# Three small moves in the front of a fused attention and mixer kernel: one weight tile's loads a step sooner, one batch's correction written ahead of two copies, and one product placed in another PSUM bank

## The chip, the cores and the metric

The kernel runs on one core of one Trainium2 chip. The metric is device time in microseconds (us) of one execution, and the median of three runs is used. One further execution was recorded by the hardware profiler; every row of the profile comes from that one, and its own time differs a little from the median (table below).

The core has engines that run independently and meet at semaphores: TensorE (PE, with its weight loads shown as PEld), VectorE (DVE), ScalarE (ACT), GpSimd (POOL) and SyncE (SP, which here only issues DMAs; ScalarE issues a few as well). Each engine takes its instructions in the order in which they were written, so an instruction that waits holds all that stand behind it on its engine.

## The reference, cut to what matters

```python
for b in range(nb):                       # lightning attention, heads of 64
    intra = einsum('bhic,bhjc->bhij', qb, kb) * Dmask
    intra = einsum('bhij,bhjd->bhid', intra, vb)
    inter = einsum('bhid,bhde->bhie', qb * lam_pow, kv_state)
    out[:, :, sl] = intra + inter
    kv_state = lam_block * kv_state + einsum('bhsd,bhse->bhde', kb * rev_pow, vb)
x = out as (B, S, H*D)                    # 4 x 768 x 512
h = (x.T @ U @ V).T                       # U: 768 x 32, V: 32 x 768, fp64 inputs
u = x + h
return u + relu(u @ w_ch1) @ w_ch2        # w_ch1: 512 x 2048, w_ch2: 2048 x 512
```

There are four batches, eight heads of 64 and 768 positions. The weights of the mixer come as 64-bit floats; the kernel turns their words into 32-bit floats with integer and float instructions of VectorE and ScalarE, and splits each into a high part, a low part and a difference, so that three products in the matmul's faster format stand for one exact one.

## The kernel before, in words

**Steps.** The attention goes by steps `s` = 0 to 23: batch `b` = s // 6 and chunk `c` = s % 6 of 128 positions. Every step is a list of pieces (`step`, L656 to L681), and this list is the order of the work: it is written out by hand, and each piece puts its instructions on the queues of several engines. For a step in the middle the pieces are, in order:

- `mix` and `turn` of an earlier batch's chunk (its correction h, and its transposition for the mixer), and `split` (the parts of the transposed chunk);
- `prep(s+1)`: PE transposes the next chunk's q and k into the PSUM tile `pqk` (L361), ScalarE copies them out as `qt` and `kt` (L367), and SP loads a further q;
- `scale(s+1)`: GpSimd multiplies q by powers of lam (L392) and the next k by others (`ks`, L381);
- `mixed` (VectorE adds h to x, L574) and `late` (ScalarE's share of the weight work);
- `intra(s)` (PE, masked scores by v into `px`, L455), `state(s)` (PE, `ks` by v into `pkv`, L427, and VectorE's new state `kv`, at a first chunk a plain copy, L433), a load of v on ScalarE's queue, and `inter(s)` (PE adds q by the state to `px`, L466; ScalarE copies `px` out as `x_nat`, L472). At c = 0 there is no state yet, so `inter` is the copy alone;
- `scores(s+1)` (PE, L408) and `masked(s+1)` (VectorE, L417), with the step's share of weight work, `aside(s)`, between them;
- `store` of a finished chunk and the load of a further k, both on SP.

**PSUM.** The front uses tiles of two banks of 512 floats per partition each: tags `pqk`, `px`, `pss` and `pm`, one buffer each. `px` holds 256 columns of 512 in each of its two banks. The product `pkv` borrows a tile (L423): `pm` up to s = 6, later `pss` at chunks 2 to 4, and `pqk` at chunks 0 and 1. In `pqk` it has to wait for ScalarE's copies of q and k.

**The correction h.** After a batch's last chunk PE computes x by U for the batch (`low`, L482) and ScalarE copies the sum out as `p_f` (L491). `next_of_low` is then called twice in the next batch's first step. The first call (`own`, L525) rounds four strips of `p_f` into `vp` on ScalarE (L528) and takes the rest on GpSimd (L529); in the list it stands behind `prep`, so behind the copies of q and k on ScalarE. The second call (`other`) sends four small DMAs from `vp` to `vp` on SP (L539). `mix` (L562) multiplies V by `vp`; the first `mix` of a batch is due in the next step, at c = 1, behind `inter`. For the last batch there is another path after the attention.

**Weight work.** `side` (L738 to L747) lists at which step each instruction group of the first weight tiles is written: U, V, and the first two of 16 tiles of w_ch1. A tile of w_ch1 has twelve groups: four fetches of 128 KB each on SP (L146), `one` (exponents, L166, with two ScalarE instructions), `mantissa` (L155), `two` (L184), `three` (L192), `four` (L197) and three for the split. The groups of one step go into `aside(s)`, after `scores(s+1)` and ahead of `masked(s+1)`, so what VectorE has there stands ahead of the mask. The first tile has its fetches at steps 8 to 11 and `one` at 12. The second has

```python
(w1_steps(1, True, True), (15, 16, 17, 18, 18, 22, 23, NS, NS, NS, NS, NS)),
```

that is fetches at 15, 16, 17 and 18, and `one` at 18 too. The buffer of the words alternates between two pools, so the second tile's fetches don't wait for the first tile's groups.

**After the attention** come the products with w_ch1 (`hidden`, L833 and L844) for the rest of the weight tiles, with results parked in DRAM, and then the products with w_ch2 (L965 to L969). They take the time from about 120 us to the end, with PE busy throughout.

Of the kernel before, what the change touches and what calls it, by code (L numbers as in the profile page):

```python
# [18 lines left out]
def kernel(  # L19
# [30 lines left out]
    B, H, S, D = q.shape  # L50
    HP = H // 2
    NT = S // P
# [7 lines left out]
    NS = B * NT  # L60
# [142 lines left out]
    def split_steps(tile_of, src, in_parts=False, scale=None, apart=False):  # L203

        st = {}

        def dst():
            if "w" not in st:
                st["w"] = wconv.tile([P, C], FP32, tag="wf", name="wf")
            return st["w"]  # L210

        def five():
            st["o"] = o = tile_of()
            st["t"] = o[:, 0, :].bitcast(FP32)
            on_scalar(lambda: nc.scalar.mul(o[:, 0, :], st["w"], NEAR))  # L215

        def six():
            w, low = st["w"], st["o"][:, 1, :]
            st["low"] = low.bitcast(FP32) if scale is None else w
            nc.vector.tensor_tensor(  # L220
                out=low if scale is None else w, in0=w, in1=st["t"], op=ALU.subtract
            )
            if scale is not None:
                on_scalar(lambda: nc.scalar.mul(low, w, scale))

        def seven():
            nc.vector.scalar_tensor_tensor(
                st["o"][:, 2, :], st["t"], -E, st["low"], ALU.mult, ALU.add
            )

        return weight_steps(dst, src, C, in_parts=in_parts, apart=apart) + [five, six, seven]
# [3 lines left out]
    def w1_steps(ft, in_parts=False, apart=False):  # L235
        def tile_of():
            w1v[ft] = w1_pool.tile([P, 3, C], F32R, tag="w1", name="w1")
            return w1v[ft]

        cols = moe_w_ch1[:, ft * P : (ft + 1) * P].rearrange("(c p) f -> p c f", p=P)  # L240
        return split_steps(tile_of, cols, in_parts, apart=apart)
# [13 lines left out]
    def two_banks(name, tag):  # L255
        return psf.tile([P, 2, N], FP32, tag=tag, name=name)
# [81 lines left out]
    st = {}  # L338
# [80 lines left out]
    def state(s):  # L419
        c = s % NT  # L420
        if c < NT - 1:
            ks, vr = st[s]["ks"], raw[s, "v"]
            pkv = two_banks("pkv", "pm" if s <= NT else "pss" if c > 1 else "pqk")[:, 0, 0 : HP * D]  # L423
            pkv = pkv.rearrange("p (a e) -> p a e", a=HP)
            for a in range(HP):
                for x in range(2):
                    nc.tensor.matmul(  # L427
                        out=pkv[half[x], a, :], lhsT=ks[:, a, x, :], rhs=vr[:, 2 * a + x, :],
                        start=True, stop=True,
                    )  # L430
            kv[s + 1] = att.tile([P, HP, D], FP32, tag="kv", bufs=2, name="kv")
            if c == 0:
                nc.vector.tensor_copy(out=kv[s + 1], in_=pkv)  # L433
            elif c > 1:
                nc.vector.tensor_tensor(out=kv[s + 1], in0=pkv, in1=st[s]["faded"], op=ALU.add)
            else:
                for a in range(HP):
                    nc.vector.scalar_tensor_tensor(
                        kv[s + 1][:, a, :], kv[s][:, a, :], lamc[:, a, :], pkv[:, a, :],
                        ALU.mult, ALU.add,  # L440
                    )
# [207 lines left out]
    for s in range(NS):  # L649
        b, c = divmod(s, NT)  # L650
        done = s - NT - 1
        more = s + 1 < NS
        turns = done > 0 and (done - 1) // TG < FG
        mixes = 0 <= done < NS - NT - 1
        rows = c == 0 and b > 0
        step = [("fade", s)] * (c > 0)  # L656
        step += [("mix", done)] * (mixes and c != 1) + [("turn", done - 1)] * turns
        step += [("split", done - 1)] * turns
        step += [("prep", s + 1)] * more
        step += [("mix", done + 1)] * (not more)  # L660
        step += [("next_of_low", b - 1)] * rows
        step += [("scale", s + 1)] * more
        step += [("mixed", done)] * (mixes and c != 1)
        step += [("late", s - 1)] * (1 < s < NT - 1 or s > NT)
        step += [("turned", done - 2)] * (done > 1 and c == 1)
        step += [("mixed", done + 1)] * (not more)
        both = [("intra", s), ("state", s)]
        step += (both if s > NT else both[::-1]) + [("next_v", s), ("inter", s)]
        step += [("next_of_low", b - 1)] * rows
        step += [("late", s)] * (s < 2 or s in (NT - 1, NT))  # L670
        step += [("turned", done - 1)] * (done > 0 and c > 0)
        step += [("mix", done), ("mixed", done)] * (mixes and c == 1)
        step += [("scores", s + 1)] * more
        step += [("low", b)] * (more and c == NT - 1)
        step += [("aside", s)] * (0 < s < NT - 2 or s > NT)
        step += [("masked", s + 1)] * more
        step += [("low_rows", b)] * (more and c == NT - 1)
        step += [("aside", s)] * (s in (0, NT - 2, NT - 1, NT))
        step += [("store", done)] * (done >= 0 and done // TG < FG)
        step += [("next_k", s)] * (s > 0)  # L680
        pieces += step  # L681
    waiting = {name: list(range(NS)) for name in "qkv"}

    def load_next(name, engine=nc.sync):
# [4 lines left out]
    run = {  # L689
        "prep": prep, "fade": fade, "scores": scores, "masked": masked, "inter": inter,  # L690
        "intra": intra, "state": state,
        "low": low, "low_rows": low_rows, "next_of_low": next_of_low, "mix": mix, "turn": turn,
        "mixed": mixed, "store": store, "next_v": next_v, "split": lambda s: splits.pop(s)(),
# [3 lines left out]
    def v_steps():  # L697

        st = {}

        def dst():
            if "v" not in st:
                st["v"] = wconv.tile([P, C], FP32, tag="wf", name="vf")[0 : 2 * R, 0:SH]
            return st["v"]

        def parts(gs):
            for half in range(2):
                rows, cols = slice(half * R, (half + 1) * R), slice(half * SH, (half + 1) * SH)
                for g in gs:
                    yield v_hl[g * R : (g + 1) * R, cols], rows  # L710

        def five():
            st["t"] = t = wconv.tile([P, C], FP32, tag="wt", name="vt")[0 : 2 * R, 0:SH]
            nc.vector.tensor_scalar(
                t.bitcast(U32), st["v"].bitcast(U32), HI, None, ALU.bitwise_and
            )
            on_scalar(high)

        def high():
            for out, rows in parts((0, 2)):  # L720
                nc.scalar.copy(out, st["t"][rows])

        def low(g, engine):
            for out, rows in parts((g,)):
                engine.tensor_tensor(
                    out=out, in0=st["v"][rows], in1=st["t"][rows], op=ALU.subtract
                )

        halves = [moe_V[:, half * SH : (half + 1) * SH] for half in range(2)]
        return weight_steps(dst, halves, SH, 2 * R, in_parts=True) + [  # L730
            five, lambda: low(1, nc.vector), lambda: low(3, nc.gpsimd),
        ]
# [6 lines left out]
    for steps, at in (  # L739
        (u_side, (-1, 1, 1, 2, 2)),  # L740
        (v_steps(), (0, 0, 3, 3, 4, 4, 4, 5, 5)),
        (w1_steps(0, True, True), (8, 9, 10, 11, 12, 14, 15, 16, 17, 17, 20, 21)),
        (w1_steps(1, True, True), (15, 16, 17, 18, 18, 22, 23, NS, NS, NS, NS, NS)),
    ):
        assert len(steps) == len(at)
        for step, n in zip(steps, at):
            side.setdefault(n, []).append(step)  # L747
# [140 lines left out]
    c0, b = NS - NT, B - 1  # L888
# [180 lines left out]
```

## Time and profile before

| | us |
|---|---|
| median of 3 runs | 659.63 |
| lowest and highest run | 659.31, 661.56 |
| the profiled execution's own time | 657.43 |
| its span, first to last instruction | 655.6 |
| PE busy | 640.6 (98%) |
| VectorE busy | 435.8 (66%) |
| ScalarE busy | 268.6 (41%) |
| GpSimd busy | 116.4 (18%) |

A row of the timeline reads: start in us, length in us, engine, line, operation, output <- inputs, shape, count, and in brackets how long the engine had been idle before it and what ended that. "SPq" and "ACTq" are instructions that issue DMAs. A row of waits reads: engine, line, what it waited for, us in total, times, and the longest. In a table of stretches PEclk is the mean share of full speed that PE's clock had in the records.

### The profile page before, as it was taken

What the parts mean: (1) busy time and instruction counts of PE and PEld (TensorE: products, weight loads), DVE (VectorE), ACT (ScalarE), POOL (GpSimd) and SP (SyncE); (2) the same over time, 40 slices, a digit from 0 to 9 for tenths busy, and PEclk for the clock granted to TensorE, in tenths of its full rate; (3) what the DMA queues carried; (4) which work ended last, traced back from release to release, by engine and by line L of the source; (5) the groups of instructions that cost most, each with busy time, mean ns of one, the idle gap of its engine ahead of it and who ended that gap; (6) DMA issues with size and microseconds to landing.
All of it is one profiled execution on the core that took longest, in us unless ns stands there. A gap on an engine that the chain in (4) does not pass through costs nothing.

```text
span 655.6 us, 13402 instructions
## 1 busy us (share of the span) xinstructions
PE 640.6 (98%) x5242; PEld 539.5 (82%) x5242; DVE 435.8 (66%) x713; ACT 268.6 (41%) x497; POOL 116.4 (18%) x104
## 2 busy tenths in 40 slices
PE   8999979999999999999999999999999999999997
PEld 7889968778888888888888888888888888888886
DVE  6766857676997777777798244585575665855854
ACT  4666756434664444444455131332232322322320
POOL 4475966331000000000000000030030210300300
PEclk9999998999999999999999999999999999999999
DMA  9989995155787556555576999865363363453521
GB/s 227 241 197 259 236 239 130 50 201 170 262 287 253 211 210 211 209 212 210 211 253 255 332 323 379 292 216 173 98 215 108 116 211 97 147 176 94 180 81 64
DMA packets 132737, 131.69 MB, mean 201 GB/s; under 512 B 81538, under 2 KB 90754, under 8 KB 132674
## 3 DMA queue, kind: packets, MB, share of 16 engines
q1 hardware_dynamic: 107552, 124.41, 58.4%
q10 hardware_dynamic: 25122, 6.42, 4.4%
q8 instruction: 41, 0.67, 0.4%
q14 instruction: 22, 0.18, 0.1%
HBM read 80.09 MB, written 50.33 MB: 199 GB/s over the span
## 4 chain that ended last, share of the span: by engine, by line
PE 93%; DVE 2%; DMA 1%; ACT 1%; issue 1%; POOL 0%; SPq 0%; ACTq 0%; DVEq 0%
PE pz L833 26%; PE pz L965 13%; PE pz L967 13%; PE pd L969 13%; PE pd L844 13%; PE px L455 3%; PE pss L408 3%; PE px L466 2%; PE pqk L361 1%; PE pkv L427 1%; PE pm L562 1%; DMA qraw<-in_q_dram 1%; PE pp L482 1%; PE pm L625 1%; DMA vp<-vp 0%
## 5 line engine op out<-in xcount | busy, mean ns | idle before, releaser
L833 PE MATMUL pz<-u_hl,w 128*128 128x512 f32 x768 | 184.5, 390 | 0.0
L833 PEld LDWEIGHTS pz<-u_hl,w 128*128 128x128 f32 x768 | 143.7, 188 | 30.0 <-ACT r L840 0.3
L967 PE MATMUL pz<-w_hl,m 128*128 128x512 f32 x384 | 148.6, 389 | 0.0
L965 PE MATMUL pz<-w_hl,m 128*128 128x512 f32 x384 | 148.2, 389 | 0.0
L969 PE MATMUL pd<-w_d,m 128*128 128x512 f32 x384 | 147.4, 389 | 0.0
L948 ACT ACTIVATE m<-rm 128x512 fp32r<-128x512 f32 x96 | 60.6, 632 | 183.1 <-PE pd L969 122.9
L949 DVE SCALAR_TENSOR_TENSOR m<-rm,m 128x512 fp32r<-128x512 f32 x96 | 71.5, 747 | 96.0 <-ACT m L948 96.0
L994 POOL TENSOR_TENSOR o<-o,u 128x512 f32<-128x512 f32 x20 | 29.7, 1521 | 433.3 <-DVE o L990 433.3
L849 DVE SCALAR_TENSOR_TENSOR r<-pd,r 128x512 f32<-128x512 f32 x96 | 61.7, 685 | 60.4 <-ACT r L840 48.2
L844 PE MATMUL pd<-u_d,w 128*128 128x512 f32 x384 | 95.9, 390 | 0.0
L969 PEld LDWEIGHTS pd<-w_d,m 128*128 128x128 f32 x384 | 72.1, 188 | 15.4 <-DVE m L950 0.3
L967 PEld LDWEIGHTS pz<-w_hl,m 128*128 128x128 f32 x384 | 72.1, 188 | 15.1
L965 PEld LDWEIGHTS pz<-w_hl,m 128*128 128x128 f32 x384 | 72.1, 188 | 14.7
L844 PEld LDWEIGHTS pd<-u_d,w 128*128 128x128 f32 x384 | 71.9, 188 | 14.8
L840 ACT ACTIVATE r<-pz 128x512 f32<-128x512 f32 x96 | 51.7, 590 | 64.4 <-PE pz L833 64.4
L950 DVE SCALAR_TENSOR_TENSOR m<-m 128x512 fp32r<-128x512 f32 x96 | 74.7, 780 | 3.0
L417 DVE TENSOR_TENSOR sm<-pss,mask 128x512 f32<-128x512 f32 x48 | 30.9, 684 | 16.7 <-PE pss L408 16.7
L215 ACT ACTIVATE w<-wf 128x512 fp32r<-128x512 f32 x32 | 20.3, 634 | 38.6 <-DVE wf L197 30.7
L455 PE MATMUL px<-vraw,sm 128*64 128x64 f32 x768 | 28.7, 229 | 5.6 <-issue 5.5
L455 PEld LDWEIGHTS px<-vraw,sm 128*64 128x64 f32 x768 | 25.8, 141 | 7.3 <-issue 5.8
L173 ACT ACTIVATE sc<-sc,ends 128x512 f32<-128x512 uint32 x30 | 21.6, 720 | 22.8 <-DVE sc L166 22.8
L408 PE MATMUL pss<-qt,kt 64*128 64x128 f32 x384 | 28.8, 289 | 0.0
(89 smaller groups left out, 608.5 us busy)
## 6 DMA issues: line engine op xcount, KB each, us to landing
r_d<-r SPq DMA_DIRECT2D x96, 256.0 KB, 2.4
rm<-r_d SPq DMA_DIRECT2D x96, 256.0 KB, 2.7
words<-in_moe_w_ch_dram SPq DMA_DIRECT2D x30, 512.0 KB, 4.3
w_d<-w SPq DMA_DIRECT2D x16, 768.0 KB, 3.4
w_hl<-w_d SPq DMA_DIRECT2D x16, 512.0 KB, 5.8
u_d<-x_nat SPq DMA_DIRECT2D x24, 256.0 KB, 4.0
u<-u_d SPq DMA_DIRECT2D x24, 256.0 KB, 4.3
qraw<-in_q_dram SPq DMA_DIRECT2D x23, 256.0 KB, 4.8
```

The lines of the kernel that those rows point to most:

```text
L408: nc.tensor.matmul(out=pss[:, x, a, :], lhsT=kt[half[x], a, :], rhs=qt[half[x], a, :], start=True, stop=True,)
L455: nc.tensor.matmul(out=px[half[t], x, a, :], lhsT=sm[:, x, a, half[t]], rhs=vr[:, 2 * a + x, :], start=(a == 0), stop=(alone and a == HP - 1),
L833: nc.tensor.matmul(out=like(acc[g][0], g), lhsT=w[:, n, ct, :], rhs=columns(uhl[g][:, n], g, ct), start=(ct == 0 and n == 0), stop=(ct == ...
L840: nc.scalar.mul(rs[g], acc[g][0], 4096.0 + 1.0)
L844: nc.tensor.matmul(out=like(acc[g][1], g), lhsT=w[:, 2, ct, :], rhs=columns(ud[g], g, ct), start=(ct == 0), stop=(ct == CT - 1),)
L849: nc.vector.scalar_tensor_tensor(rs[g], acc[g][1], 4096.0, rs[g], ALU.mult, ALU.add)
L948: nc.scalar.activation(out=m[:, 0], in_=r, func=AF.Relu, scale=NEAR)
L949: nc.vector.scalar_tensor_tensor(m[:, 1], r, 0.0, hi, ALU.max, ALU.subtract)
L950: nc.vector.scalar_tensor_tensor(m[:, 2], hi, E, low, ALU.mult, ALU.subtract)
L965: nc.tensor.matmul(out=pz, lhsT=m[:, 0, cols], rhs=hl[:, 0], start=first, stop=False)
L967: nc.tensor.matmul(out=pz, lhsT=m[:, 1, cols], rhs=hl[:, 1], start=False, stop=end)
L969: nc.tensor.matmul(out=pd, lhsT=m[:, 2, cols], rhs=dd, start=first, stop=end)
```

## The change

Three edits. (A) At the first chunk of the third and fourth batch (s = 12 and 18) `pkv` is written to the unused columns 256 to 511 of the first bank of `px`, in place of a tile with the tag `pqk`. (B) At s = 6 the first call of `next_of_low` is written ahead of `prep(7)` rather than behind it; at s = 12 and 18 it stays where it was. (C) The second tile's four fetches are written at steps 14, 15, 16 and 17 rather than 15 to 18; `one` stays at 18.

```diff
         if c < NT - 1:
             ks, vr = st[s]["ks"], raw[s, "v"]
-            pkv = two_banks("pkv", "pm" if s <= NT else "pss" if c > 1 else "pqk")[:, 0, 0 : HP * D]
+            if c == 0 and s > NT:
+                pkv = st[s]["px"][:, 0, HP * D : 2 * HP * D]
+            else:
+                tag = "pm" if s <= NT else "pss" if c > 1 else "pqk"
+                pkv = two_banks("pkv", tag)[:, 0, 0 : HP * D]
             pkv = pkv.rearrange("p (a e) -> p a e", a=HP)
...
         step += [("split", done - 1)] * turns
+        step += [("next_of_low", b - 1)] * (s == NT)
         step += [("prep", s + 1)] * more
         step += [("mix", done + 1)] * (not more)
-        step += [("next_of_low", b - 1)] * rows
+        step += [("next_of_low", b - 1)] * (rows and s > NT)
         step += [("scale", s + 1)] * more
...
-        (w1_steps(1, True, True), (15, 16, 17, 18, 18, 22, 23, NS, NS, NS, NS, NS)),
+        (w1_steps(1, True, True), (14, 15, 16, 17, 18, 22, 23, NS, NS, NS, NS, NS)),
```

## The prediction

> **What bounds the kernel now.** I read the busy times first, then the waits of PE in the front (20 to 120 us), then the timeline around each of these waits.
>
> ```profile
> PE 640.6 (98%) x5242; PEld 539.5 (82%) x5242; DVE 435.8 (66%) x713; ACT 268.6 (41%) x497; POOL 116.4 (18%) x104
> ...
> PE px L455 <- issue: 5.5, 3, 4.8
> PE pm L562 <- DMA vp<-vp: 1.2, 1, 1.2
> PE pkv L427 <- issue: 0.3, 2, 0.2
> ```
>
> PE is busy for 640.6 us of the 655.6 us span, so nearly only PE's idle time, or time in which it runs slowly, is there to be won. The three wait rows come from the answer on PE's waits between 20 and 120 us, and they are in effect the three edits: up to 4.8 us ahead of one `intra` (edit C), 1.2 us in the first `mix` (edit B), two stalls of about 0.2 us ahead of `pkv` (edit A). Behind the front PE hardly waits, so I take it that what the front gains arrives at the end undiminished: the products that follow hang on PE and on engines that move with it, not on a fixed hour.
>
> **Edit A, `pkv` into `px`'s bank at s = 12 and 18.** No instruction is added or taken away; the eight matmuls no longer wait for the copy `kt`.
>
> ```profile
> 63.83 0.59 ACT L367 COPY kt<-pqk 128x512 f32<-128x512 f32 x1
> ...
> 64.52 0.69 PE L427 MATMUL pkv<-vraw,ks 128*64 128x64 f32 x16 [0.19 <-issue]
> ...
> 65.25 0.42 DVE L433 COPY kv<-pkv 128x256 f32<-128x256 f32 x1 [0.53 <-PE pkv L427]
> ...
> 65.66 0.59 ACT L472 COPY x_nat<-px 128x512 f32<-128x512 f32 x1
> ...
> 67.14 1.24 PE L455 MATMUL px<-vraw,sm 128*64 128x64 f32 x32
> ...
> 69.50 0.78 PE L562 MATMUL pm<-vp 64*128 64x256 f32 x4
> ...
> L539 SPq DMA_DIRECT2D vp<-vp x1: 585/585/585, 67.8 to 67.8; - x1
> ...
> DMA to landing us min/median/max: 1.8/1.8/1.8
> ...
> 91.94 0.69 PE L427 MATMUL pkv<-vraw,ks 128*64 128x64 f32 x16 [0.16 <-issue]
> ```
>
> At s = 12 `kt` ends at 63.83 + 0.59 = 64.42 and `pkv` starts at 64.52 after 0.19 us of idling; at s = 18 it idled 0.16 us. If everything behind moved along, A would bring 0.35 us. But what is late next stands in the same rows: `mix` at 69.50 needs four strips of `vp`. The last strip's DMA (the answer on the tile `vp`) starts at 67.8 and lands 1.8 us later, at 69.6, so `mix` begins with the strip not quite there and takes 0.78 us. The strips hang on ScalarE behind `kt`, which A does not move. I take 0 for A. Ends: a gain of 0.35 and a loss of 0.1, the latter since the changed `pkv` shares `px`'s bank, so ScalarE's `x_nat` (65.66) now also waits for VectorE's copy `kv`, which ends at 65.25 + 0.42 = 65.67. Behind it on ScalarE stand the next split and the next copies of q and k; the next writer of `px` comes only at 67.14, 0.9 us after `x_nat` ends at 66.25.
>
> [...]
>
> **Edit B, ScalarE's four casts ahead of `qt` and `kt` at s = 6.** The four casts move past two copies on ScalarE; GpSimd's four subtractions and SP's four DMAs keep their places in their queues but are released sooner.
>
> ```profile
> 34.39 0.27 ACT L491 COPY p_f<-pp 128x128 f32<-128x128 f32 x1
> ...
> 35.03 0.58 ACT L367 COPY qt<-pqk 128x512 f32<-128x512 f32 x1 [0.37 <-PE pqk L361]
> ...
> 35.51 0.59 ACT L367 COPY kt<-pqk 128x512 f32<-128x512 f32 x1
> ...
> 36.12 0.62 ACT L528 CAST vp<-p_f 32x128 fp32r<-32x128 f32 x2
> ...
> 36.41 1.16 PE L408 MATMUL pss<-qt,kt 64*128 64x128 f32 x16
> 36.50 2.02 POOL L529 TENSOR_TENSOR vp<-p_f,vp 32x128 fp32r<-32x128 f32 x4 [2.03 <-ACT vp L528]
> ...
> 36.97 2.79 SPq L539 DMA_DIRECT2D vp<-vp  x4
> ...
> 39.17 3.01 DMA vp<-vp
> ...
> 40.05 0.69 PE L466 MATMUL px<-kv,qs 64*64 64x64 f32 x32
> ...
> 42.23 0.50 PE L562 MATMUL pm<-vp 64*128 64x256 f32 x3 [1.17 <-DMA vp<-vp]
> ```
>
> (The row without an engine is from the chain of work that ended last.) `p_f` ends at 34.66. Today the casts follow `kt` and start at 36.12; then they start at about 34.68. Two take 0.62 us, so the first is done at 34.99 and the four at 35.93. GpSimd's chain starts at 35.05 rather than 36.50, 1.45 us sooner, and with it SP's DMAs: the last strip, which today is on its way from 39.17 to 42.18, would land at about 40.73.
>
> The price: `qt` starts at 35.95 rather than 35.03, `kt` follows 0.48 us later as it does today (35.03 to 35.51) and ends at 35.95 + 0.48 + 0.59 = 37.02. `scores(7)`, which PE began at 36.41, now waits for `kt` until about 37.05: 0.64 us lost, and everything of the step behind it moves by that. `inter(7)`, today 40.05 to 40.74, then ends at 41.38. By then the strips are there, so `mix` runs through; four of its matmuls need about 0.4 us (today's last three took 0.50 with their loads) and it ends at 41.78 rather than at 42.73. Gain: 42.73 - 41.78 = 0.95 us; I take 0.9. Ends: 1.58 us if `scores(7)` is not held (0.95 + 0.64), and a loss of 0.64 us if the strips land later by as much as PE comes later, which could only come from SP's queue, where the load of q that `prep(7)` issues stands ahead of them. GpSimd's next product, q by powers, is queued behind the subtractions: they end at 35.05 + 2.02 = 37.07 and `qt` at 36.53, both ahead of today's 38.52.
>
> **Edit C, the second tile's fetches one step sooner.** One DMA of 128 KB leaves step 18 and one joins step 14; nothing else moves. At s = 18 `one` stands on VectorE directly behind the last fetch's own step, and ahead of `masked(19)`.
>
> ```profile
> 92.66 0.42 DVE L433 COPY kv<-pkv 128x256 f32<-128x256 f32 x1 [0.53 <-PE pkv L427]
> ...
> 94.04 0.42 PE L361 MATMUL pqk<-ident,kraw 64*128 64x64 f32 x8
> ...
> 95.64 0.58 SPq L146 DMA_DIRECT2D words<-in_moe_w_ch_dram  x1
> ...
> 98.10 0.43 DVE L166 TENSOR_SCALAR sc<-words 128x512 uint32<-128x512 uint32 x1 [5.01 <-DMA words<-in_moe_w_ch_dram]
> 98.44 1.28 DVE L417 TENSOR_TENSOR sm<-pss,mask 128x512 f32<-128x512 f32 x2
> ...
> 99.23 1.98 PE L455 MATMUL px<-vraw,sm 128*64 128x64 f32 x32 [4.76 <-issue]
> ...
> 94.50:99.20 4.70, 0.00 (x0) 0.00 (x1) 1.10 (x3) 1.72 (x4) 3.20 (x3) 0.74 0.63 173
> 99.20:103.60 4.40, 4.37 (x84) 4.17 (x86) 1.98 (x6) 1.22 (x3) 1.46 (x2) 0.51 0.43 97
> ...
> 70.03 1.14 PE L408 MATMUL pss<-qt,kt 64*128 64x128 f32 x16
> ...
> 103.61 1.06 PE L408 MATMUL pss<-qt,kt 64*128 64x128 f32 x16
> ...
> L146 SPq DMA_DIRECT2D words<-in_moe_w_ch_dram x1: 2170/2170/2170, 86.0 to 86.0; - x1
> ...
> DMA to landing us min/median/max: 6.1/6.1/6.1
> ```
>
> VectorE is done with `kv` at 93.08. Its next instruction, L166, needs words whose fetch SP issues only at 95.64, behind the four strips; they land at 98.10. The mask (98.44) is queued behind L166, and `intra(19)` behind the mask, so PE, which finished its transposes at 94.46, starts at 99.23. The stretch from 94.50 to 99.20 has no PE work at all (the columns are length, busy time of PE, PEld, DVE, ACT and POOL, then PEclk, DMA share and GB/s). It has a second cost: in the next 4.4 us PEclk is 0.51, and `intra` takes 1.98 us where the same 32 matmuls took 1.24 us at s = 13.
>
> With C the last fetch is the one written at step 17. The fetch there today starts at 86.0 and lands 6.1 us later, at 92.1 (the last two rows of the fence), ahead of 93.08, so L166 does not wait. VectorE then does L166 until 93.5, and the mask can start when `scores(19)` ends.
>
> For the size I lay step 18 beside step 12, which has the same pieces and `one` of the first tile at the same place, with its words already landed. From `pkv` to the `scores` two steps on: 64.52 to 70.03 is 5.51 us at s = 12, and 91.94 to 103.61 is 11.67 us at s = 18. The difference, 6.16 us, is idle time (99.23 - 94.46 = 4.77) and half clock (the rest, 1.39). What is late next is again `mix`: the last strip of `vp`, whose row shows
>
> ```profile
> L539 SPq DMA_DIRECT2D vp<-vp x2: 585/585/585, 94.3 to 95.0; - x2
> ...
> DMA to landing us min/median/max: 1.9/2.0/2.1
> ```
>
> starts at 95.0 and lands by 97.1. At s = 12 `mix` came 69.50 - 64.52 = 4.98 us behind `pkv`, which gives 96.92 here; a wait of up to 0.2 us. I take 6.1 us. Ends: 4.77 us if the half clock came anyway, 6.3 us with A's share on top. On SP the store and the loads behind the fetch in step 18 go out sooner; in step 14 a store and a load of k go out later by its issue, 2.2 us where the row shows one (2170 ns). The loads are two steps and more ahead of their use, which hides it as in steps 15 to 17; without that cover it is the last rival below.
>
> **The sum.** 0 + 0.9 + 6.1 = 7.0 us. The profiled execution would take 657.43 - 7.0 = 650.4 us. It is 2.2 us below the median of the runs; against the median the forecast is 659.63 - 7.0 = 652.6 us. The ends add up to 4.77 - 0.64 - 0.1 = 4.0 us (655.6) and 6.3 + 1.58 = 7.9 us (651.7; A's gain is in the 6.3 for one of its two places and doubtful at the other).
>
> **The rivals.**
>
> *B brings nothing.* If `scores(7)` loses its 0.64 us and the strips come no sooner than 42.18, `mix` ends where it ended, and 6.1 us remain: 653.5. For it: ScalarE's queue is the only thing I moved, and SP's DMAs take 2.79 us for four. Against it: GpSimd's chain had waited for the casts alone.
>
> *The half clock stays out of the sum.* The clock's halving may not have been in the runs of the median: then C is worth 4.77 and the sum is 5.7, 654.0. Against it: the profiled execution, which has the half clock, is faster than the median. [...] The trace agrees that a pause of 4.77 us is followed by 0.51; no run here shows one that is not.
>
> *The pause moves.* If the mask comes early but `vp`'s strips, now with PE right behind them, or the loads of q and k land some 3 us later than read, C is worth about 3 us: 655.7.
>
> *The edits do nothing.* If L166 waits as long for another of the four fetches, only B is left: 658.7. The rows speak against it: the third fetch lands at 92.1.
>
> *Slower: the DMA engines become the bound in steps 14 to 17.*
>
> ```profile
> 72.30:76.60 4.30, 4.30 (x128) 4.06 (x126) 3.98 (x7) 3.16 (x9) 4.30 (x5) 1.00 1.13 269
> ...
> qraw<-in_q_dram SPq DMA_DIRECT2D x23, 256.0 KB, 4.8
> ...
> words<-in_moe_w_ch_dram SPq DMA_DIRECT2D x8, 128.0 KB, 5.1
> ```
>
> In the stretch of step 14 the DMA share is 1.13 at 269 GB/s. Each step has three loads and a store of the size in the q row, 256 KB, about 1.05 MB in 4.3 us. With 128 KB more (the last row), a step of 1.18 MB takes 4.4 us at that rate, 0.1 us more, and the loads run ahead by two steps or more, so nothing shows. To end 0.5% slower than before, these four steps would have to lose 7.0 + 3.3 = 10.3 us, 2.6 us each: 1.18 MB in 6.9 us, 171 GB/s. From that rate down it decides, and the time is 663 or more. [...]
>
> **How the numbers follow.** Forecast 0.70 (its own range 650.8 to 654.4, from the ends of B and A and the spread of the runs); B nothing 0.13; half clock out 0.05; pause moved 0.06; nothing 0.03; slower 0.03. About 0.5% (3.3 us) is what a measurement of this kernel can tell from no change. Faster by more, below 656.3: the first four, 0.94, from which I keep back 0.02 for their ends; same 0.05; slower 0.03. The range goes from 650.2, the upper sum of 7.9 with the 1.5 us that the median may come nearer to the profiled execution's time, to 655.8, which takes in the third rival.
>
> **What would show it.** After: no idle of PE above 0.5 us between 90 and 105; L166 of the second tile without a wait; PEclk near 1.00 there; `scores(7)` about 0.6 us later, `mix` of s = 7 without the 1.2 us; at s = 12 and 18 no idle before L431 but a `mix` that waits for `vp`. I would be wrong if VectorE's L166 still waits, if PE's wait for `vp` at s = 7 stays, or if waits for loads of q, k or v appear in steps 14 to 20.

## The result, and the profile after

| us | before | after |
|---|---|---|
| median of 4 runs each | 660.60 | 650.76 |
| lowest and highest run | 659.31, 662.20 | 649.45, 651.64 |
| the profiled execution's own time | 657.43 | 651.64 |
| its span | 655.6 | 649.8 |

The changed kernel takes 0.9848 of the time before, with a 95% interval of 0.9817 to 0.9879. The forecast was 652.6 us, a ratio of 0.9893 to its median of 659.63. The two profiled executions lie closer together than the medians, 5.8 us apart; what is in these 5.8 us stands in the section on why the prediction was right. The median of 650.76 us lies at the lower end of the forecast: just below its own range of 650.8 to 654.4, and above the lower end of the whole range, 650.2.

The page of the profile after has these lines of busy time and of PE's clock (40 slices of the span, nine tenths and more in every one), and PE's waits between 20 and 120 us (columns: engine, line, what it waited for, us in total, times, the longest):

```profile
PE 639.3 (98%) x5242; PEld 538.5 (83%) x5242; DVE 435.9 (67%) x713; ACT 268.1 (41%) x497; POOL 116.6 (18%) x104
...
PEclk9999999999999999999999999999999999999999
...
PE px L470 <- issue: 1.5, 2, 0.8
PE px L459 <- issue: 0.7, 2, 0.4
PE pkv L431 <- issue: 0.6, 2, 0.3
PE pss L408 <- ACT kt L367: 0.4, 1, 0.4
```

Gone are the two large waits of before, 4.8 us ahead of an `intra` and 1.2 us for `vp`. What is left are pieces of 0.8 us and less. The largest, in `inter` (L470), is new.

**Step s = 6 and 7 (edit B).** The timeline after:

```profile
34.27 1.26 ACT L532 CAST vp<-p_f 32x128 fp32r<-32x128 f32 x4
...
34.65 2.15 POOL L533 TENSOR_TENSOR vp<-p_f,vp 32x128 fp32r<-32x128 f32 x4 [0.97 <-ACT vp L532]
...
35.16 1.10 PE L459 MATMUL px<-vraw,sm 128*64 128x64 f32 x32
35.24 3.02 SPq L543 DMA_DIRECT2D vp<-vp  x4
...
36.04 0.59 ACT L367 COPY kt<-pqk 128x512 f32<-128x512 f32 x1
...
36.68 1.16 PE L408 MATMUL pss<-qt,kt 64*128 64x128 f32 x16 [0.42 <-ACT kt L367]
...
40.94 0.50 PE L566 MATMUL pm<-vp 64*128 64x256 f32 x4
...
41.28 1.05 PE L408 MATMUL pss<-qt,kt 64*128 64x128 f32 x16
```

And two rows of before that weren't shown, the `intra` of s = 6 and the `scores` of s = 8:

```profile
35.38 1.10 PE L455 MATMUL px<-vraw,sm 128*64 128x64 f32 x32
...
42.46 1.16 PE L408 MATMUL pss<-qt,kt 64*128 64x128 f32 x16
```

The four casts now run in one go from 34.27, ahead of `kt`, which ends at 36.63; `scores(7)` waits 0.42 us for it. In return `mix` (40.94) has all its strips and runs through, four matmuls in 0.50 us, and `scores(8)` starts at 41.28 rather than at 42.46.

**Steps s = 12 and 18 (edits A and C).** The timeline after:

```profile
63.44 0.63 PE L431 MATMUL px<-vraw,ks 128*64 128x64 f32 x15
...
68.36 0.61 PE L566 MATMUL pm<-vp 64*128 64x256 f32 x4
...
68.72 1.13 PE L408 MATMUL pss<-qt,kt 64*128 64x128 f32 x16
...
91.31 1.15 PE L459 MATMUL px<-vraw,sm 128*64 128x64 f32 x32
...
92.29 0.64 PE L431 MATMUL px<-vraw,ks 128*64 128x64 f32 x16
...
93.32 0.42 DVE L166 TENSOR_SCALAR sc<-words 128x512 uint32<-128x512 uint32 x1
...
94.07 1.29 DVE L417 TENSOR_TENSOR sm<-pss,mask 128x512 f32<-128x512 f32 x2 [0.33 <-PE pss L408]
...
94.25 0.57 ACT L476 COPY x_nat<-px 128x512 f32<-128x512 f32 x1
...
94.87 1.09 PEld L459 LDWEIGHTS px<-vraw,sm 128*64 128x64 f32 x32 [0.24 <-ACT x_nat L476]
...
96.37 0.69 PE L431 MATMUL pkv<-vraw,ks 128*64 128x64 f32 x16 [0.28 <-issue]
...
97.61 0.51 PE L566 MATMUL pm<-vp 64*128 64x256 f32 x4
...
97.96 1.05 PE L408 MATMUL pss<-qt,kt 64*128 64x128 f32 x16
```

Both `pkv` (63.44 and 92.29) start without idle time. L166, `one` of the second tile, no longer waits for its words, and the mask follows at 94.07. Two small waits are new: `intra(19)` at 94.87 for `x_nat`, 0.24 us, and the next `pkv` at 96.37, 0.28 us. Four stretches of the profile after follow; the last two are the ones that the prediction shows of before (length, busy time of PE, PEld, DVE, ACT, POOL, then PEclk, DMA share, GB/s):

```profile
80.00:84.00 4.00, 3.25 (x93) 2.97 (x90) 2.33 (x4) 1.50 (x3) 3.49 (x3) 1.00 1.01 265
84.00:88.00 4.00, 3.27 (x98) 2.93 (x96) 3.78 (x5) 1.91 (x4) 2.80 (x3) 1.00 1.15 295
94.50:99.20 4.70, 4.32 (x114) 3.85 (x111) 3.21 (x9) 4.57 (x11) 4.55 (x6) 1.00 0.72 173
99.20:103.60 4.40, 4.40 (x131) 4.16 (x130) 3.53 (x7) 2.93 (x8) 4.40 (x4) 1.00 1.10 274
```

Where PE stood idle for 4.70 us from 94.50 on and then ran at 0.51 of its clock, it is busy for 4.32 of 4.70 us, at full clock. In the first two stretches, steps 16 and 17, PE lacks 0.7 us each. These are the pauses of `inter`:

```profile
82.20 0.68 PE L470 MATMUL px<-kv,qs 64*64 64x64 f32 x26 [0.76 <-issue]
...
87.32 0.34 PE L470 MATMUL px<-kv,qs 64*64 64x64 f32 x7 [0.73 <-issue]
```

They fall into the middle of a group of 32 matmuls that has already begun, and the profile shows nothing that they wait for.

**Behind the front.** The first product with w_ch1 starts 5.65 us sooner than before, and the span ends 5.8 us sooner. (One row of each, before and after.)

```profile
120.40 1.89 PE L833 MATMUL pz<-u_hl,w 128*128 128x512 f32 x7
```

```profile
114.75 1.89 PE L838 MATMUL pz<-u_hl,w 128*128 128x512 f32 x7
```

### The profile page after: what moved, and what is told of

Same layout as the page of the kernel before. It is cut to its first block, busy times and chain, and to the rows that moved or that the text cites. A ratio compares the mean times of both kernels' runs of the same rounds, so it can differ in the third digit from the quotient of the medians.

```text
span 649.8 us, 13407 instructions
## 1 busy us (share of the span) xinstructions
PE 639.3 (98%) x5242; PEld 538.5 (83%) x5242; DVE 435.9 (67%) x713; ACT 268.1 (41%) x497; POOL 116.6 (18%) x104
## 4 chain that ended last, share of the span: by engine, by line
PE 94%; ACT 2%; DMA 1%; DVE 1%; issue 1%; ACTq 0%; DVEq 0%
PE pz L838 26%; PE pz L972 13%; PE pz L970 13%; PE pd L974 13%; PE pd L849 13%; PE px L459 4%; PE pss L408 3%; PE px L470 2%; PE pqk L361 2%; PE pkv L431 1%; PE pm L566 1%; DMA qraw<-in_q_dram 1%; PE pp L486 1%; DMA kraw<-in_k_dram 1%; PE pm L629 1%
## 5 line engine op out<-in xcount | busy, mean ns | idle before, releaser
L392 POOL TENSOR_TENSOR qs<-qt,powq 128x512 f32<-128x512 f32 x20 | 26.0, 1300 | 15.3 <-ACT qt L367 15.1
```

## The experiments

Ratios are to the kernel before, measured beside each group on the same chip, with 95% intervals. Each run also gives the mean granted clock of its TensorE; the kernel before has 0.990 to 0.997 in all of its 60 runs beside the experiments. An estimate from two lengths that the profiles show: 3.4 us at 0.50 (the kernel with the fetch ahead, 44.30 to 47.70) in 650 us make 1 - 0.5 x 3.4 / 650 = 0.997, and 6.7 us (before, 0.50 from 96.80 to 103.50) make 0.995.

### One part alone, and two of them

A alone, on the kernel before:

```diff
+            if c == 0 and s > NT:
+                pkv = st[s]["px"][:, 0, HP * D : 2 * HP * D]
+            else:
...
```

> Edit A alone. Theory: no idle ahead of `pkv` at s = 12 and 18, but what is won there (0.19 and 0.16 us) is given back one step later, in `mix` on the strips of `vp` or in `intra` on ScalarE's `x_nat`: ratio 1.000 (0 to -0.35 us). Rival, A is slower since `x_nat` waits for VectorE's copy out of the same bank: ratio 1.001 and a wait of PE px on ACT x_nat. Rival, A holds the 2.8 us that the forecast lacks: ratio 0.995.

Measured: 1.0008 (0.9983 to 1.0032), 660.01 us beside 658.84. A by itself brings nothing that can be measured; the interval, some 1.6 us to either side, can't tell 0 from the 0.35 us that were the upper end. In its profile the loss that the prediction had named is there, at s = 12: ScalarE's `x_nat` waits for VectorE's `kv`, which reads the same bank. A pause of 0.48 us in the middle of `intra(12)` made `pkv` and `kv` late, and no wait of PE for `x_nat` follows.

```profile
65.98 0.58 ACT L476 COPY x_nat<-px 128x512 f32<-128x512 f32 x1 [0.50 <-DVE kv L437]
```

B alone, on the kernel before:

```diff
+        step += [("next_of_low", b - 1)] * (s == NT)
         step += [("prep", s + 1)] * more
...
-        step += [("next_of_low", b - 1)] * rows
+        step += [("next_of_low", b - 1)] * (rows and s > NT)
```

> Edit B alone. Theory: the wait of 1.2 us in `mix` at s = 7 is gone, `scores(7)` is held 0.5 to 0.6 us by `kt`, the `scores` behind `mix` come 0.95 us sooner against the start of `intra(6)`; the pause of 4.8 us at step 19 stays. Ratio 0.9985 (-0.95 us). Rival, B brings nothing since the strips come no sooner: ratio 1.000. Rival, B holds the 2.8 us that the forecast lacks: ratio 0.994.

Measured: 0.9971 (0.9947 to 0.9995), 1.9 us less with 0.3 to 3.5. The forecast's 0.9 us lies in it, and the 0.994 of the second rival doesn't. In its profile PE's wait for `vp` is gone and 0.6 us for `kt` have come; the span is 0.8 us shorter. The clocks point to more than that in some runs: 13 of the 60 runs of before have 0.993 or less, by that estimate 9 us of half clock and more, and 7 of the 12 runs of A alone, but none of the 12 with B alone.

C alone, on the kernel before:

```diff
-        (w1_steps(1, True, True), (15, 16, 17, 18, 18, 22, 23, NS, NS, NS, NS, NS)),
+        (w1_steps(1, True, True), (14, 15, 16, 17, 18, 22, 23, NS, NS, NS, NS, NS)),
```

> Edit C alone. Theory of the prediction: it carries nearly all, 4.77 us of idle time ahead of `intra(19)` and 1.4 us of half clock, so the profile has no idle of PE above 0.5 us at step 19, PEclk 1.00 there, and the span is 6.1 us shorter. The medians of the changed kernel and the kernel before lie 9.8 us apart, 2.8 us more than forecast; if that goes with the pause (runs of before lose more behind it than the profiled one did), the ratio here is about 0.987 (-8.5 us or more). Rival, C is worth only the 6.1 us and the rest lies with A or B: ratio 0.991. Rival, the pause moves to another wait: ratio 0.995 or nearer to 1.

Measured: 0.9901 (0.987 to 0.9932), 6.5 us less with 4.5 to 8.6. This is nearly the whole gain, as forecast; that the 2.8 us beyond the forecast lie with C isn't shown. The strips of `vp` now hold up PE for 1.71 us at s = 7, more than in the profile of before:

```profile
41.74 0.50 PE L562 MATMUL pm<-vp 64*128 64x256 f32 x3 [1.71 <-DMA vp<-vp]
```

B and C, without A (on the changed kernel, A undone):

```diff
-            if c == 0 and s > NT:
-                pkv = st[s]["px"][:, 0, HP * D : 2 * HP * D]
-            else:
-                tag = "pm" if s <= NT else "pss" if c > 1 else "pqk"
-                pkv = two_banks("pkv", tag)[:, 0, 0 : HP * D]
+            pkv = two_banks("pkv", "pm" if s <= NT else "pss" if c > 1 else "pqk")[:, 0, 0 : HP * D]
```

> The changed kernel with edit A undone. Theory: the same time as the changed kernel within what can be measured, ratio to the kernel before 0.985 as there, since A is worth 0 to 0.35 us. Rival, A is worth 2.8 us: ratio 0.989.

Measured: 0.9884 (0.9848 to 0.992), 7.6 us less with 5.3 to 10.0. The interval takes in both measurements of the changed kernel (0.9848 above, 0.9895 below). Its timeline at s = 18 is what explains A:

```profile
92.93 1.15 PE L455 MATMUL px<-vraw,sm 128*64 128x64 f32 x32
...
94.27 0.69 PE L427 MATMUL pkv<-vraw,ks 128*64 128x64 f32 x16 [0.19 <-issue]
...
95.87 0.57 ACT L472 COPY x_nat<-px 128x512 f32<-128x512 f32 x1
...
98.01 0.69 PE L427 MATMUL pkv<-vraw,ks 128*64 128x64 f32 x16
...
99.61 1.14 PE L408 MATMUL pss<-qt,kt 64*128 64x128 f32 x16
```

From `intra(18)` to ScalarE's `x_nat` are 95.87 - 92.93 = 2.94 us here, without A, and 94.25 - 91.31 = 2.94 us with A. From `intra(18)` to `scores(20)` are 6.68 us here and 6.65 us with A. So at s = 18 A does take the 0.19 us ahead of `pkv` away, but ScalarE's queue goes its own pace from `kt` on, and PE meets it again at `x_nat` and at the next copies.

### The changed kernel again

> The changed kernel once more, with more runs of both. Theory: the forecast of -7.0 us was right in size (ratio 0.9894) and the first ratio of 0.9848 stood on few runs of a kernel whose runs spread by several us; with more runs it comes to 0.987 to 0.990. Rival, there is a real gain of 2.8 us beyond the forecast: the ratio stays at 0.985.

Measured: 0.9895 (0.987 to 0.992), 651.69 us beside 658.61, 6.9 us less. The first result's 0.9848 stood on four runs of each kernel; the kernel before has run from 655.5 to 663.2 us over the experiments, so four of its runs can shift a ratio by some tenths of a per cent. In this second profile the pauses in `inter` are not there. Another one is, of 1.1 us, in the middle of the transposes:

```profile
PE pqk L361 <- issue: 1.1, 1, 1.1
```

So the same kernel has them at other places in another execution. No one edit is needed for them either: the profiles of A alone, B alone and C alone each have one, of 0.48, 0.70 and 0.78 us, in the middle of an `intra`.

### What the pause at s = 19 hung on

`one` of the second tile a step later, fetches left at 15 to 18 (on the kernel before):

```diff
-        (w1_steps(1, True, True), (15, 16, 17, 18, 18, 22, 23, NS, NS, NS, NS, NS)),
+        (w1_steps(1, True, True), (15, 16, 17, 18, 19, 22, 23, NS, NS, NS, NS, NS)),
```

> The kernel before with one step moved: the fetches stay at 15 to 18 and `one` of the second tile goes from step 18 to 19. This takes away the wait of L166 without an earlier fetch. Theory: the pause of 4.8 us at step 19 is gone as with edit C, PEclk stays at 1.00, L166 does not wait, ratio 0.990 as edit C alone. Rival, the earlier fetch itself matters (loads of a busier stage move): ratio clearly different from edit C alone, or PE waits for loads. Rival, L166 waits at step 19 for the words just the same: ratio 1.000.

Measured: 0.9938 (0.9912 to 0.9964), 4.1 us less with 2.4 to 5.8. That is less than the 0.990 expected and than the 6.5 us of C alone; the two intervals overlap, so whether the earlier fetch is worth something of its own stays open.

```profile
93.27 1.29 DVE L417 TENSOR_TENSOR sm<-pss,mask 128x512 f32<-128x512 f32 x2 [0.68 <-PE pss L408]
...
94.06 1.24 PE L455 MATMUL px<-vraw,sm 128*64 128x64 f32 x32
...
94.89 0.58 SPq L146 DMA_DIRECT2D words<-in_moe_w_ch_dram  x1
...
97.70 0.85 DVE L166 TENSOR_SCALAR sc<-words 128x512 uint32<-128x512 uint32 x1
```

The pause at s = 19 is gone although the fetch goes out as late as before: `intra(19)` starts at 94.06, before the fetch has even been issued. So it was VectorE's queue, in which the mask stood behind L166, that carried the DMA's lateness to PE. The profiled run took 651.6 us at clock 1.00. Six of the twelve runs have a clock of 0.997 or less, which none of the ten runs of the changed kernel has.

The last fetch left in step 18, but written ahead of the four DMAs of the strips (on the kernel before):

```diff
+        step += [("aside", "ahead")] * (s == NS - NT)
         step += [("next_of_low", b - 1)] * rows
...
-        (w1_steps(1, True, True), (15, 16, 17, 18, 18, 22, 23, NS, NS, NS, NS, NS)),
+        (w1_steps(1, True, True), (15, 16, 17, "ahead", 18, 22, 23, NS, NS, NS, NS, NS)),
```

> The kernel before with the fetch of step 18 written ahead of the four DMAs of `other`, not behind: on SP's queue it goes out about 91 rather than at 95.6 and lands at 95 to 96, so L166 waits some 2 to 3 us rather than 5 and PE's pause is shortened to 2 to 3 us. What is told apart is the half clock. [...] If each pause costs clock in proportion, PEclk behind it is 0.5 for a part of the stretch and the gain is 2.3 to 3 us.

Measured: 0.9949 (0.9927 to 0.9971), 3.4 us less with 1.9 to 4.8. L166 still waits 1.48 us (2 to 3 were expected), and PE 1.89 us behind it. The place behind the strips' DMAs was thus only a part of the fetch's lateness; the step in which it is written was the rest. The same profile shows something else, at s = 7:

```profile
43.90 0.50 PE L562 MATMUL pm<-vp 64*128 64x256 f32 x3 [1.96 <-DMA vp<-vp]
...
100.80 1.24 PE L455 MATMUL px<-vraw,sm 128*64 128x64 f32 x32 [1.89 <-ACT kt L367]
```

```profile
40.90:44.30 3.40, 1.44 (x43) 1.15 (x41) 0.86 (x4) 1.65 (x5) 3.11 (x3) 1.00 0.73 164
44.30:47.70 3.40, 3.40 (x45) 3.30 (x43) 2.08 (x4) 0.60 (x1) 0.00 (x0) 0.50 0.85 213
```

The strips of `vp` held PE for 1.96 us. In the 3.4 us around this wait PE was busy for 1.44 us, and in the next 3.4 us the clock is 0.50. The second wait of nearly the same length, 1.89 us at 100.80, was followed by no such stretch (PEclk 1.00 from 100.00 to 104.00). So beside the wait itself there was a second cost here, up to 1.7 us (an estimate, half of the 3.4 us), which comes in some executions only: six of this kernel's twelve runs have a clock of 0.997 or less, the others 0.999 and 1.000.

All four fetches two steps sooner still (on the changed kernel):

```diff
-        (w1_steps(1, True, True), (14, 15, 16, 17, 18, 22, 23, NS, NS, NS, NS, NS)),
+        (w1_steps(1, True, True), (12, 13, 14, 15, 18, 22, 23, NS, NS, NS, NS, NS)),
```

> The changed kernel with the second tile's fetches at steps 12 to 15 in place of 14 to 17. In its profile PE pauses twice, 0.76 and 0.73 us, within a group of `inter` matmuls at steps 16 and 17, with no wait that the profile shows, in stretches with a DMA share above 1.0. If the fetches of these steps cause the pauses, they are gone here or move to steps 12 to 15, and the time is up to 1.5 us shorter (0.9977 of the changed kernel). If not, pauses of this kind stand at the same places of the program with other lengths, and the time is the same as the changed kernel's.

Measured: 0.9893 (0.9865 to 0.992), 651.70 us beside the changed kernel's 651.69. One step is enough; no further gain can be measured. Of the two pauses in `inter` none is left in this profile. But PE now waits about as long ahead of two `scores`, at steps 14 and 15, where the profile names VectorE's `kv` and ScalarE's `x_nat`:

```profile
77.93 1.13 PE L408 MATMUL pss<-qt,kt 64*128 64x128 f32 x15 [0.68 <-DVE kv L439]
...
82.96 1.13 PE L408 MATMUL pss<-qt,kt 64*128 64x128 f32 x15 [0.71 <-ACT x_nat L476]
```

That the fetches cause the pauses in `inter` doesn't follow: the changed kernel's second profile lacks them with the fetches at 14 to 17.

### What the strips at s = 7 cost

A and C, with B undone:

```diff
-        step += [("next_of_low", b - 1)] * (s == NT)
...
-        step += [("next_of_low", b - 1)] * (rows and s > NT)
+        step += [("next_of_low", b - 1)] * rows
```

> The changed kernel with edit B undone. Two profiles without B showed more than the 1.2 us wait in the first `mix`: 1.7 us, and 2.0 us followed by 3.4 us of half clock. Theory now: beside its 0.95 us, B takes away this half clock in the runs that have it, so this kernel is slower than the changed one by 1 us in most runs and by 2.5 us and more in some, whose mean clock is 0.997 rather than 1.00; ratio to the kernel before 0.991 to 0.992. Rival, B is worth its 0.95 us in every run: the mean clock is 1.00 in all runs, ratio 0.991 and no wider spread than the changed kernel's.

Measured: 0.9892 (0.9871 to 0.9914), 652.62 us. `mix` waits again. The ratio is below the 0.991 to 0.992 that both theory and rival had, and no higher than the changed kernel's 0.9895, so by time alone B's share can't be told from nothing here. By the clock it can: two of five runs have a clock of 0.996 and 0.997; the other three have 0.999 and 1.000.

```profile
42.25 0.50 PE L566 MATMUL pm<-vp 64*128 64x256 f32 x3 [1.85 <-DMA vp<-vp]
```

The opposite of B, on the changed kernel: the casts of s = 6 not ahead of `prep(7)`, but at the end, behind `inter(6)`:

```diff
-        step += [("next_of_low", b - 1)] * (s == NT)
...
         step += (both if s > NT else both[::-1]) + [("next_v", s), ("inter", s)]
-        step += [("next_of_low", b - 1)] * rows
+        step += [("next_of_low", b - 1)] * (rows + (s == NT))
```

> The changed kernel with edit B turned round: at s = 6 the four casts are written behind ScalarE's copy `x_nat`, later even than before. They start about 1.9 us later than before, so the strips land about 1.9 us later and PE waits about 3 us in the first `mix`. Theory: such a wait halves PE's clock for one window of 3.4 us in nearly every run (mean clock 0.997 and less); against the changed kernel with B undone 1.9 us of waiting and 1.4 to 1.7 us of half clock more, ratio to the kernel before 0.996. [...]

Measured: 0.9934 (0.9908 to 0.9959), 655.98 us. That is 3.4 us more than with B merely undone, on the same chip, where the theory had 3.3 to 3.6, 1.9 of them waiting; the ratio itself lies below the theory's 0.996. Four of its six runs have a clock of 0.994 to 0.997. In the profiled one, which kept its clock, the wait is shorter than the 3 us expected, but longer than the 1.96 us that were followed by half clock above:

```profile
45.03 0.50 PE L566 MATMUL pm<-vp 64*128 64x256 f32 x3 [2.30 <-DMA vp<-vp]
```

Why it kept its clock, no run shows.

Taken together: of the 32 runs of kernels that are rid of the pause at s = 19 but have the strips where they were or later (C alone, `one` at 19, A and C, the strips late), 15 have a clock of 0.997 or less. Of the 26 runs with B and C both (the changed kernel in both measurements, B and C, the fetches at 12 to 15, and the kernel below) none has: all lie at 0.999 or 1.000. With C alone the six runs at 0.999 and more have a median of 651.3 us, and the three at 0.997 one of 655.1 us. By the estimate above, 3.4 us at half clock cost up to 1.7 us; what else those runs lost, no profile shows.

### A further version

The second tile's remaining groups written sooner, so that VectorE has less to do right behind the front (on the changed kernel):

```diff
-        (w1_steps(1, True, True), (14, 15, 16, 17, 18, 22, 23, NS, NS, NS, NS, NS)),
+        (w1_steps(1, True, True), (14, 15, 16, 17, 18, 20, 21, 22, 23, 23, NS, NS)),
```

> The changed kernel with the second tile's later groups sooner too: `mantissa` at 20, `two` 21, `three` 22, `four` and `five` 23, and only the last two behind the attention. In the changed kernel PE waits 0.9 us at 129.7 for VectorE's `x_nat` (L574), which is queued behind `three`, `four` and `six` of this tile. Theory: this wait is gone or halved and nothing else moves, -0.5 to -0.9 us against the changed kernel, too little for the ratio to show (0.988 to 0.989) but plain in the waits of PE. Rival, VectorE becomes late in steps 20 to 23 and `intra` waits for the mask: slower than the changed kernel by 1 us or more.

Measured: 0.9874 (0.9852 to 0.9896), 651.64 us beside 659.76. The interval overlaps the changed kernel's; it isn't shown to be better. PE's waits from 20 to 140 us show why little was left. In the changed kernel PE waits 1.3 us in this stretch for `x_nat` on VectorE, as before:

```profile
PE put L607 <- DVE x_nat L574: 1.3, 2, 0.9
```

```profile
PE px L459 <- ACT kt L367: 1.2, 1, 1.2
...
PE px L459 <- ACT u_hl L643: 0.4, 1, 0.4
PE put L607 <- DVE x_nat L574: 0.4, 1, 0.4
```

Of these 1.3 us 0.9 are saved, and 1.6 us of waits for ScalarE have come in the last steps of the front, where the moved groups now stand.

## Why the prediction was right, and where not

**The bound and how the gain is carried.** That PE bounds the kernel and that the front's gain arrives undiminished held: 5.65 us at the first product with w_ch1, 5.8 us at the end.

**Edit A.** Zero agrees with what could be measured; the step that was to give the gain back was wrong. I named `mix`, late for want of `vp`'s strips. At s = 18 `mix` (97.61) runs through. There the 0.16 us are given back at `x_nat` and at the next `pkv`, because ScalarE's queue, which A leaves alone, is the one that PE meets next: 2.94 us from `intra(18)` to `x_nat` with and without A. At s = 12 the pair of profiles doesn't show it given back: from `intra(12)` to `scores(14)` are 70.03 - 63.18 = 6.85 us before and 68.72 - 62.25 = 6.47 us after. The seven profiles with A have 6.47 to 7.30 us there and the six without 6.72 to 7.31, pauses inside matmul groups included, so a gain of 0.2 us at this place is neither shown nor ruled out.

**Edit B.** From the starts of `intra(6)` to `scores(8)`: 42.46 - 35.38 = 7.08 us before, 41.28 - 35.16 = 6.12 us after, 0.96 us gained where 0.95 were worked out. Over all profiles this stretch is 5.64 to 6.53 us in the six with B and 7.07 to 8.81 us in the seven without. The loss at `scores(7)` was 36.68 - 35.16 less 36.41 - 35.38, 0.49 us for a forecast 0.64: the casts started at 34.27, 0.4 us sooner than I had them, while the step as a whole ran only 0.2 us sooner (35.16 for 35.38). The strips were no longer waited for. The rival "B brings nothing" falls by the row of `mix` without a wait. What the sum didn't have is half clock behind the strips' wait, as in the profile with the fetch ahead (0.50 for 3.4 us behind a wait of 1.96 us). It wasn't in the trace of before, where the wait was 1.17 us and the clock stayed at 1.00 (42.40 to 45.80).

**Edit C.** From `pkv` of s = 18 to `scores(20)`: 97.96 - 92.29 = 5.67 us, where it had been 11.67; 6.0 us gained for 6.16 by the comparison with step 12 and 6.1 in the sum. L166 without a wait, no idle of PE above 0.28 us between 90 and 105, and full clock are as forecast. The two new waits, 0.24 and 0.28 us, stand where I had a wait of up to 0.2 us of `mix` for the strips.

**The sum, in the two profiles.** `intra(6)` -0.22 (35.16 for 35.38; ahead of B's first effect on PE), B -0.96, s = 8 to 14 with A at s = 12 -0.13 (`scores(14)` 70.03 to 68.72, less 1.18), s = 14 to 18 +1.66, C -6.0, and the rest to the end of the span -0.15: -5.8 us. The +1.66 us are the step that no part of the prediction had: 0.76 + 0.73 us are the two pauses in `inter`, and some 0.2 us I didn't follow. Without the pauses the pair would differ by 7.3 us, and the forecast was 7.0.

**The medians.** The second measurement, 6.9 us, meets the forecast of 7.0; the first, 9.8 us, is 2.8 us beyond it. I put the difference down to few runs, though not all of it need be that: A, B and C alone, at the middle of their ratios +0.5, -1.9 and -6.5 us, add up to 7.9 us less, and B and C together gave 7.6 (5.3 to 10.0). Half clock at s = 7, which no term of the sum had, is a candidate for what goes beyond 7.0; no run settles its share. That the second measurement meets the middle of the forecast so closely is in part luck.

**The other rivals.** *Half clock out of the sum*: all 60 runs of before lie at a clock of 0.997 or less, and the changed kernel's at 0.999 and more, so the halving was in the runs. C took most of it away (six of the nine runs of C alone are at 0.999 or more), C and B together all of it. *Pause moves* and *the edits do nothing*: no pause above 0.28 us at its place. *DMA engines the bound*: DMA share reaches 1.15 at 295 GB/s in step 17, more than I had read for step 14, and no load was waited for; apart from the two pauses PE ran through.

## What to carry to other kernels

Look for the instruction that merely stands behind the late one: it was the mask, queued on VectorE behind weight work whose words came late, that stopped PE, and moving either the weight work or the fetch cures it. A wait that is removed is worth what the next queue allows, so follow each engine's queue and not only the transfer you already suspect; A's gain at s = 18 was given back by ScalarE (2.94 us to `x_nat` with and without A). And where PE waits for 2 us, look at the clock over many runs: one trace can show such a wait at full clock (A and C, 1.85 us, clock 1.000) while other runs of the same kernel have less (0.996 and 0.997).

## What the runs showed of the hardware that was not expected

A wait of about 2 us was followed by half clock in one place and not in others. In the kernel with the fetch ahead the strips held PE for 1.96 us: from 40.90 to 44.30 PE was busy for 1.44 us, from 44.30 to 47.70 the clock was 0.50, and from 47.70 to 51.10 it was 1.00 again. In the same profile it was 1.00 behind the wait of 1.89 us (100.00 to 104.00). With A and C it was 1.00 behind 1.85 us, and with the strips late 1.00 behind 2.30 us (40.80 to 51.00 in both). C alone, with a wait of 1.71 us, has a mean clock of 0.999 over its whole profile. So the length of the wait alone didn't decide here: 1.96 us was followed by half clock and 2.30 us wasn't. What did decide, these runs don't show.

The pause at s = 19 in the profile of before is longer, 4.70 us without PE work from 94.50 on. There the clock was 1.00 from 92.50 to 96.70, 0.50 from 96.80 to 103.50, and 1.00 from 103.60 to 108.00. It was thus halved 2.3 us into the pause and stayed so for 4.3 us of the work behind it. All 60 runs of this kernel beside the experiments have a mean clock of 0.997 or less.

PE pauses of 0.2 to 1.1 us lie inside groups of matmuls that have already begun, with nothing that the profile shows as their cause: 0.76 and 0.73 us in `inter` in the changed kernel's first profile, 1.1 us in the transposes of its second. The place differs between these two executions of one kernel, but some places come again in other kernels: the profile with B and C has 0.36 and 0.45 us at the same two places in `inter`, and C alone and A with C both have 0.8 us ahead of the last 18 matmuls of `intra(12)`. The run with the fetches at 12 to 15 is the only one that tried something on them, and it decides nothing. Their cause stays open.
